# Full-width value products with a block of ones beside V, row sums on the other partition half, and reordered first pairs, in a banded-attention and feed-forward kernel

## The chip, the cores and the metric

One core of one Trainium2 chip. The metric is the time in microseconds (us) of one execution of the whole program, as the device measures it. Where a ratio is given, it is the mean time of one kernel's fast runs over the mean time of the other's in the same rounds on the same chip, with a 95% interval; it is therefore not quite the ratio of the medians that are quoted beside it. Single figures such as "the logarithm took 714 ns" are from one profiled execution of the kernel named.

## The reference, cut to what matters

```python
def _attn_ref(q, k, v, global_idx):        # B=8, H=8, S=576, D=64, 8 global positions
    scores = (1 / np.sqrt(D)) * np.matmul(q, k.transpose(0, 1, 3, 2))
    mask = np.abs(pos[:, None] - pos[None, :]) <= 32           # a band ...
    mask = mask | is_global[:, None] | is_global[None, :]      # ... and global rows, columns
    scores = np.where(mask, scores, -1e9)
    attn = np.exp(scores - np.max(scores, axis=-1, keepdims=True))
    attn = attn / (np.sum(attn, axis=-1, keepdims=True) + 1e-09)
    return np.matmul(attn, v)

def _moe_ref(x, w_in, w_out, s, b):        # 4608 tokens, 512 -> 2048 -> 512
    r = np.maximum(x @ w_in, 0.0)
    g = s * (r * r) + b
    return g @ w_out                       # x is the attention's output, heads side by side
```

## The kernel before

The attention runs over 32 pairs of heads (eight batches, four pairs each). Each pair passes eight steps. In steps 0 to 4 one of five chunks of keys is handled: a score matmul `pss`, an exponential `e` on ScalarE, a masked product `em` on VectorE. In step 6 come the value products `po`. The normalisation of that pair then runs inside the chunks of the *next* pair: a logarithm `ln` of the row sums at step 1, its reciprocal exponential `rep` at step 3, and the product `xt` on VectorE in step 4. Between all this, one "quantum" of feed-forward work per step fills TensorE: 16 quanta `psh` (products with `w_in`, each evicted by a ReLU on ScalarE and squared on VectorE), then 16 quanta `pso` (products with `w_out`), of which every fourth is evicted. From pair 9 on the pairs take turns in this: two that run mostly `psh`, two that run mostly `pso`.

```python
def pv(p, parts=(0, 1)):                       # value products, 28 matmuls, 64 columns wide
    for part in parts:                         # part 0: V, part 1: row sums
        for c in range(NCH):
            for a, n, x in pieces(part * LQ, c):
                for hh in range(2):            # the two heads of the pair
                    nc.tensor.matmul(
                        po[D * hh : D * hh + D, a : a + n],
                        onesb[:] if part else vring[:, p % NV, c, hh],
                        emt[(p, c)][:, hh, x : x + n], ...)

def norm_steps(p):
    def sums():                                # attention of the global rows
        nc.vector.tensor_reduce(out=gs[:, hp], in_=..., axis=AX.X, op=OP.add)
        ...
    def s1():
        nc.scalar.activation(ln[:], po[:, LQ : 2 * LQ], AF.Ln)          # 128 x 640
        later.append(sums)
    def s2():
        nc.scalar.activation(rep[:], ln[:], AF.Exp, scale=-1.0)
        later.append(lambda: nc.vector.tensor_tensor(                   # 128 x 600
            out=view(xt[:, hp, x0:], ...), in0=halves(po[:, 0:LQ]),
            in1=halves(rep[:]), op=OP.mult))
    return [s1, s2]

def run_pair(p, nq, extra):
    for s in range(8) if p > 4 else range(NCH, 8):
        prev, later[:] = list(later), []
        if s < NCH:
            qk(p, s)                           # pss, e; em goes to `later`
            if s in (1, 3):
                step()                         # s1 at step 1, s2 at step 3
        ...
        elif s == 6:
            pv(p)
            pending.extend(norm_steps(p))
        for f in prev:                         # VectorE work of the step before
            f()
        if s == 6 and p + 1 < NSIX:
            put_v(None, p + 1)                 # the global rows of V, by SyncE's DMA queue
        for f in extra.get(s, ()):             # adds and releases: one at step 4, ...
            f()
        Q(nq[s])                               # a quantum of the feed-forward
```

The `po` tile has one buffer: the value products of a pair may not start before the `xt` of the pair ahead has read it.

The softmax here doesn't subtract the row's maximum and nothing guards it: scores larger than these inputs give would overflow.

## Time and profile before

| | before |
|---|---|
| median of 3 runs | 378.12 us (377.26 to 379.49) |
| span of the profiled run | 377.1 us |
| TensorE, VectorE, ScalarE busy | 91%, 63%, 61% |
| a pair in the middle, from its last value product to that of the next pair | 9.02 us, most of them; 9.3 to 9.9 us where `psh` runs |

Two more views are needed later. The first is the page's account of the chain of work that ended last, by engine and by line. It reads backwards from the last instruction, always to what released it: in nearly two thirds of the time the end waited for TensorE.

```profile
PE 63%; ACT 10%; issue 8%; DVE 8%; DMA 5%; POOL 3%; SPq 1%; POOLq 0%; ACTq 0%; DVEq 0%
```

The second is the cost of the two instructions that the change splits, from the page's groups (line, engine, operation, output and inputs, count, total busy us, mean ns, idle time before).

```profile
L539 DVE TENSOR_TENSOR xt<-po,rep 128x600 bf16<-128x600 f32 x32 | 25.0, 782 | 6.1 <-ACT rep L537 5.4
...
L533 ACT ACTIVATE ln<-po 128x640 f32<-128x640 f32 x32 | 22.8, 714 | 1.9 <-PE po L502 1.7
```

### The profile page before, as it was taken

Reading aid. Unit: us, or ns where it says so; the run is one execution under the profiler, and the core shown is the slowest. Engines: PE = TensorE matmul, PEld = TensorE weight load, DVE = VectorE, ACT = ScalarE, POOL = GpSimd, SP = SyncE. Lnnn points to the kernel's source line nnn. Section 1 sums busy time; section 2 is a strip of 40 time slices with the busy share of each in tenths; the row PEclk is TensorE's granted clock in tenths of the full one; section 3 lists DMA queues with packets and bytes.
Section 4 is the critical chain, followed back from the end, with each engine's and each line's share of the span. In section 5 each row is a group of like instructions: output and inputs, shape, how many; then the busy total and the mean of one; then the engine's idle time right before and its main releaser. Section 6 shows DMA issues by size and latency. Waiting matters only on the chain.

```text
span 377.1 us, 7687 instructions
## 1 busy us (share of the span) xinstructions
PE 342.7 (91%) x2707; PEld 183.3 (49%) x2743; DVE 238.5 (63%) x634; ACT 228.8 (61%) x441; POOL 74.9 (20%) x156
## 2 busy tenths in 40 slices
PE   4777697389999999999999999999999999999995
PEld 1344443235545554556765555555556754444442
DVE  3667756357788879866776786667656753432421
ACT  8448767375588458745874687479658841611610
POOL 6664193102213331011202110201020010000000
PEclk9969989889999999999999999999999999999999
DMA  7999489979878866659976998786424002002002
GB/s 133 201 211 217 74 139 212 192 162 180 176 159 190 191 161 117 119 129 209 191 167 146 214 202 136 169 188 124 107 91 71 2 28 86 0 29 85 1 28 83
DMA packets 125831, 50.15 MB, mean 133 GB/s; under 512 B 113512, under 2 KB 118632, under 8 KB 125792
## 3 DMA queue, kind: packets, MB, share of 16 engines
q1 hardware_dynamic: 117040, 37.34, 49.0%
q0 software_dynamic: 8544, 12.03, 16.0%
q8 instruction: 21, 0.34, 0.4%
q10 hardware_dynamic: 208, 0.29, 0.3%
q14 instruction: 18, 0.15, 0.1%
HBM read 42.26 MB, written 9.44 MB: 137 GB/s over the span
## 4 chain that ended last, share of the span: by engine, by line
PE 63%; ACT 10%; issue 8%; DVE 8%; DMA 5%; POOL 3%; SPq 1%; POOLq 0%; ACTq 0%; DVEq 0%
PE pso L588 31%; PE psh L573 21%; PE po L502 6%; PE pss L476 4%; ACT r L580 4%; DMA natv<-in_v_dram 3%; DVE g L583 2%; ACT e L480 2%; ACT rep L537 1%; PE pst L196 1%; DVE em L483 1%; DMA vring<-gvx 1%; DMA wst<-in_moe_w_out_dram 1%; ACT qbd L231 1%; DVE xt L539 1%
## 5 line engine op out<-in xcount | busy, mean ns | idle before, releaser
L573 PE MATMUL psh<-xt,win_t 128*128 128x512 bf16 (+4 forms) x690 | 141.7, 344 | 2.3 <-POOL xt L550 1.0
L588 PE MATMUL pso<-wout_t,g 128*128 128x512 bf16 x559 | 135.7, 379 | 2.0 <-issue 1.6
L580 ACT ACTIVATE r<-psh 128x512 bf16<-128x512 f32 x144 | 89.3, 620 | 64.1 <-PE psh L573 62.6
L480 ACT ACTIVATE e<-pss 128x384 bf16<-128x384 f32 (+1 forms) x160 | 77.0, 488 | 62.6 <-PE pss L476 62.6
L573 PEld LDWEIGHTS <-win_t 128*128 128x128 bf16 x704 | 64.9, 99 | 57.0 <-issue 5.6
L583 DVE TENSOR_TENSOR g<-r 128x512 bf16<-128x512 bf16 x144 | 62.6, 435 | 35.4 <-ACT r L580 33.3
L588 PEld LDWEIGHTS <-g 128*128 128x128 bf16 x576 | 54.8, 98 | 59.5
L483 DVE TENSOR_TENSOR em<-e,mask 128x384 bf16<-128x384 bf16 (+1 forms) x160 | 57.0, 357 | 18.5 <-ACT e L480 17.6
L476 PE MATMUL pss<-qbd,kt 128*128 128x384 bf16 (+1 forms) x160 | 50.7, 321 | 5.7 <-DVE qbd L428 2.4
L602 DVE SCALAR_TENSOR_TENSOR osb<-pso,s_bc,bias_row 128x512 f32<-128x512 f32 x28 | 21.0, 750 | 38.1 <-PE pso L588 38.1
L550 POOL COPY xt<-xg 128x4 bf16 x64 | 14.6, 229 | 115.1 <-DVE xt L539 111.4
L216 POOL CAST vring<-natv 128x640 bf16<-128x640 f32 x24 | 17.7, 739 | 69.8 <-DMA natv<-in_v_dram 21.8
L502 PE MATMUL po<-em,vring 128*64 128x160 bf16 (+3 forms) x448 | 21.9, 229 | 8.0 <-DMA vring<-gvx 6.1
L539 DVE TENSOR_TENSOR xt<-po,rep 128x600 bf16<-128x600 f32 x32 | 25.0, 782 | 6.1 <-ACT rep L537 5.4
L502 PEld LDWEIGHTS <-vring 128*64 128x64 bf16 x448 | 17.0, 113 | 19.8 <-issue 9.1
L476 PEld LDWEIGHTS <-kt 128*128 128x128 bf16 x160 | 15.7, 99 | 20.4 <-DVE qbd L428 5.5
L537 ACT ACTIVATE rep<-ln 128x640 f32<-128x640 f32 x32 | 24.4, 762 | 0.0
L533 ACT ACTIVATE ln<-po 128x640 f32<-128x640 f32 x32 | 22.8, 714 | 1.9 <-PE po L502 1.7
L204 DVE COPY qbd<-pst 64x600 bf16<-64x600 bf16 x48 | 22.3, 465 | 0.3
L502 PE MATMUL po<-em,onesb 128*64 128x160 bf16 (+2 forms) x448 | 19.9, 225 | 0.0
L465 DVE COPY qbd<-pst 64x600 bf16<-64x600 bf16 x8 | 6.2, 774 | 21.1 <-ACT qbd L465 21.1
L182 ACT CAST natbk<-natk 120x640 bf16<-120x640 f32 x24 | 18.2, 760 | 0.0
(99 smaller groups left out, 224.5 us busy)
## 6 DMA issues: line engine op xcount, KB each, us to landing
natv<-in_v_dram SPq DMA_DIRECT2D x55, 150.0 KB
out_dram<-osb SPq DMA_DIRECT2D x28, 256.0 KB
natk<-in_k_dram SPq DMA_DIRECT2D x47, 150.0 KB
natq<-in_q_dram SPq DMA_DIRECT2D x47, 150.0 KB
wst<-in_moe_w_out_dram POOLq DMA_DIRECT2D x8, 512.0 KB, 6.5
win_t<-in_moe_w_in_dram POOLq DMA_DIRECT2D x2, 1024.0 KB
wout_t<-in_moe_w_out_dram POOLq DMA_DIRECT2D x4, 512.0 KB
out_dram<-osbh SPq DMA_DIRECT2D x8, 256.0 KB
```

What stands on the lines that cost most here:

```text
L204: nc.vector.tensor_copy(out=view(qbufs[p % 3][r, hh], [P, NCH], [HB + NG, 2], [1, HB]), in_=view(ps[r], [P, NCH], [HB, 2], [1, HB]),)
L476: nc.tensor.matmul(ps[:], ktile[p][:, P * c : P * c + P], qbufs[p % 3][:, :, LO[c] : HI[c]])
L480: nc.scalar.activation(e[:], ps[:], AF.Exp, scale=SCALE)
L483: later.append(lambda: nc.vector.tensor_mul(em[:], e[:], masks[c]))
L502: nc.tensor.matmul(po[D * hh : D * hh + D, a : a + n], onesb[:] if part else vring[:, p % NV, c, hh], emt[(p, c)][:, hh, x : x + n], start ...
L533: nc.scalar.activation(ln[:], po[:, LQ : 2 * LQ], AF.Ln)
L537: nc.scalar.activation(rep[:], ln[:], AF.Exp, scale=-1.0)
L539: lambda: nc.vector.tensor_tensor(out=view(xt[:, hp, x0:], [KC, NCH], [HB, 2], [1, HB]), in0=halves(po[:, 0:LQ]), in1=halves(rep[:]), op=O ...
L573: nc.tensor.matmul(psh[:, d0 : d0 + n], win_t[:, a, f * P : f * P + P], xt[:, a, x0 : x0 + n], start=(a == 0 and j == 0), stop=(a == 3), s ...
L580: nc.scalar.activation(r[:], psh[:], AF.Relu)
L583: later.append(lambda g=g, r=r: nc.vector.tensor_mul(g[:], r[:], r[:]))
L588: nc.tensor.matmul(pso[:], gl[f][:, u * P : u * P + P], wout_t[:, f], start=(f == 0), stop=(f == 15),)
```

## The change

Its intent: of the 28 half-width matmuls of a pair's value products, half compute only row sums. If each head's stationary operand holds its 64 columns of V *and* 64 columns of ones, 14 full-width matmuls give both, and TensorE need not switch its tiling for them. Head 0 has the ones first, so its values land on partitions 64 to 127 and its row sums on 0 to 63; head 1 the other way round. The heads thus lie swapped by halves, which swapped rows of `w_in` undo. The price: the row sums of a head lie on the other half than its values, and in other columns for the two heads, so the logarithm and `xt` each become two instructions on 64 partitions. So do the small reciprocal and product of the global rows, which VectorE does once for a batch, in the first pair of the next one.

```diff
-    vring = const.tile([P, NV, NCH, 2, D], BF16)
+    vring = const.tile([P, NV, NCH, 2, 2 * D], BF16)
...
-        for part in parts:
+        for hh in parts:
             for c in range(NCH):
-                for a, n, x in pieces(part * LQ, c):
-                    for hh in range(2):
-                        nc.tensor.matmul(
-                            po[D * hh : D * hh + D, a : a + n],
-                            onesb[:] if part else vring[:, p % NV, c, hh], ...
+                for a, n, x in pieces(hh * LQ, c):
+                    nc.tensor.matmul(
+                        po[:, a : a + n], vring[:, p % NV, c, hh], emt[(p, c)][:, hh, x : x + n], ...
...
+        own = [slice(D, P), slice(0, D)]
         def s1():
-            nc.scalar.activation(ln[:], po[:, LQ : 2 * LQ], AF.Ln)
+            for hh in range(2):
+                nc.scalar.activation(
+                    ln[own[hh]], po[own[1 - hh], LQ * hh : LQ * hh + LQ], AF.Ln
+                )
...
+            def scaled():
+                for hh in range(2):
+                    nc.vector.tensor_tensor(
+                        out=view(xt[own[hh], hp, x0:], ...),
+                        in0=halves(po[own[hh], LQ * hh : LQ * hh + LQ]),
+                        in1=halves(rep[own[hh]]), op=OP.mult,
+                    )
```

The rest, in short: `w_in` is loaded in four pieces with its halves swapped; the start is reordered (q is rounded before buffers are cleared, the band is built by GpSimd, the global rows are evicted by ScalarE); in pairs 5 to 7 the global V rows are put in place by VectorE instead of by a transfer; and three feed-forward quanta move from the tail into batch 1:

```diff
             if s == 6 and p + 1 < NSIX:
-                put_v(None, p + 1)
+                put_v(V, p + 1)
...
-            nq = [0, 1, 1, 1, 0, 1, 1, 1] if hp else [0, 0, 0, 0, 0, 0, 1, 2]
+            nq = [0, 1, 1, 1, 0, 1, 1, 2] if hp else [0, 0, 0, 0, 0, 0, 1, 2]
```

More of the change, by code (lines that the diff above doesn't have):

```diff
@@ L215, in cast_v @@
     def cast_v(eng, p):
-        eng(out=vring[:, p % NV], in_=natv[:, p % NV])
+        eng(
+            out=view(vring[:, p % NV, 0, 0, D:], [4 * D, NCH], [1, 2 * D]),
+            in_=natv[:, p % NV].rearrange("p c h d -> p c (h d)"),
+        )
     nc.scalar.add_instruction(
@@ L231, in clear @@
         nc.scalar.copy(out=ap, in_=view(zero[0 : ap.shape[0]], [0, n]))
-    for t in qbufs[:2]:
-        clear(t[0:D, 1], LQ)
-        clear(t[D:P, 0], LQ)
-    clear(natv[0:NG].rearrange("p n c h d -> p (n c h d)"), NV * NCH * 2 * D)
-    clear(qbufs[2][0:D, 1], LQ)
-    clear(qbufs[2][D:P, 0], LQ)
+    nc.vector.memset(qbufs[0][0:D, 1], 0.0)
+    nc.vector.memset(qbufs[0][D:P, 0], 0.0)
+    nc.scalar.copy(out=six["q"][:NP6, 0].rearrange("p h j d -> p (h j d)"), in_=six0["q"])
     for t in "kq":
@@ L246 @@
     nc.vector.memset(half[D:P], float(S))
-    onesb = const.tile([P, D], BF16)
-    nc.vector.memset(onesb[:], 1.0)
     load_v(nc.sync, 0)
@@ L272 @@
     )
+    nc.vector.tensor_copy(
+        out=six["k"][:NP6, 0].rearrange("p h j d -> p (h j d)"), in_=six0["k"]
+    )
+    for t in qbufs[1:]:
+        nc.vector.memset(t[0:D, 1], 0.0)
+        nc.vector.memset(t[D:P, 0], 0.0)
     grow = [const.tile([P, 1], mybir.dt.uint32, name=f"grow{i}", tag=f"grow{i}") for i in range(4)]
@@ L283 @@
     rows_of(0)
-    nc.vector.tensor_copy(
-        out=six["k"][:NP6, 0].rearrange("p h j d -> p (h j d)"), in_=six0["k"]
-    )
-    nc.scalar.copy(out=six["q"][:NP6, 0].rearrange("p h j d -> p (h j d)"), in_=six0["q"])
     gfs = {}
@@ L326 @@
         nc.gpsimd.memset(t[0:NG, WIN : WIN + P], 1.0)
+    nc.gpsimd.memset(kidx[0:NG], 100000.0)
+    nc.gpsimd.memset(iot[:, GAP : GAP + NG], 100000.0)
+    band = const.tile([P, WM], FP32)
+    nc.gpsimd.tensor_tensor(out=band[:], in0=iot[:], in1=iot[:], op=OP.mult)
+    nc.gpsimd.tensor_scalar(
+        out=band[:], in0=band[:], scalar1=(float(WIN) + 0.5) ** 2, scalar2=None, op0=OP.is_le
+    )
     gather(0, "kqv")
@@ L343 @@
     for j in range(2):
-        nc.gpsimd.dma_start(
-            out=win_t[:, :, 1024 * j : 1024 * j + 1024],
-            in_=w_in2[:, :, 1024 * j : 1024 * j + 1024],
-        )
+        for hh in range(2):
+            f = slice(1024 * j, 1024 * j + 1024)
+            r, o = slice(D * hh, D * hh + D), slice(D - D * hh, P - D * hh)
+            nc.gpsimd.dma_start(out=win_t[o, :, f], in_=w_in2[r, :, f])
         if j == 0:
@@ L387, in evac @@
             def evac():
-                nc.vector.tensor_copy(out=gkt[bb][:], in_=ps[:, 0])
+                eng = nc.vector.tensor_copy if bb else nc.scalar.copy
+                eng(out=gkt[bb][:], in_=ps[:, 0])
                 for hh in range(2):
                     r = slice(D * hh, D * hh + D)
-                    nc.vector.tensor_copy(out=gqd[bb % 2][r, hh], in_=ps[r, 1])
+                    eng(out=gqd[bb % 2][r, hh], in_=ps[r, 1])
             later.append(evac)
@@ L404, in move @@
             later.append(
-                lambda: nc.vector.tensor_copy(
+                lambda: nc.scalar.copy(
                     out=gvx[bb][:, 512 * i : 512 * i + 512],
@@ L417, in put_v @@
         (eng or nc.sync.dma_start)(
-            out=vring[0:NG, p % NV].rearrange("g c h d -> g c (h d)"),
+            out=view(vring[0:NG, p % NV, 0, 0, D:], [4 * D, NCH], [1, 2 * D]),
             in_=view(g, [0, NCH], [1, 2 * D]),
@@ L496, in pv @@
         po, started = otile[p]
-        for part in parts:
+        for hh in parts:
             for c in range(NCH):
-                for a, n, x in pieces(part * LQ, c):
-                    for hh in range(2):
-                        key = (a // 512, hh)
-                        nc.tensor.matmul(
-                            po[D * hh : D * hh + D, a : a + n],
-                            onesb[:] if part else vring[:, p % NV, c, hh],
-                            emt[(p, c)][:, hh, x : x + n],
-                            start=key not in started, stop=(part == 1 or c == NCH - 1),
-                            skip_group_check=True,
-                        )
-                        started.add(key)
+                for a, n, x in pieces(hh * LQ, c):
+                    key = a // 512
+                    nc.tensor.matmul(
+                        po[:, a : a + n], vring[:, p % NV, c, hh], emt[(p, c)][:, hh, x : x + n],
+                        start=key not in started, stop=(hh == 1 or c == NCH - 1),
+                        skip_group_check=True,
+                    )
+                    started.add(key)
     def norm_steps(p):
@@ L528, in sums @@
                 xgs[bi] = xg
-                nc.vector.reciprocal(out=rec[:], in_=gs[:, :, 1])
-                nc.vector.tensor_tensor(out=xg[:], in0=gs[:, :, 0], in1=rec[:], op=OP.mult)
+                for hh in range(2):
+                    nc.vector.reciprocal(out=rec[own[hh]], in_=gs[own[1 - hh], :, hh])
+                for hh in range(2):
+                    nc.vector.tensor_tensor(
+                        out=xg[own[hh]], in0=gs[own[hh], :, hh], in1=rec[own[hh]], op=OP.mult
+                    )
         def s1():
-            nc.scalar.activation(ln[:], po[:, LQ : 2 * LQ], AF.Ln)
+            for hh in range(2):
+                nc.scalar.activation(
+                    ln[own[hh]], po[own[1 - hh], LQ * hh : LQ * hh + LQ], AF.Ln
+                )
             later.append(sums)
@@ L537, in s2 @@
             nc.scalar.activation(rep[:], ln[:], AF.Exp, scale=-1.0)
-            later.append(
-                lambda: nc.vector.tensor_tensor(
-                    out=view(xt[:, hp, x0:], [KC, NCH], [HB, 2], [1, HB]),
-                    in0=halves(po[:, 0:LQ]), in1=halves(rep[:]), op=OP.mult,
-                )
-            )
+            def scaled():
+                for hh in range(2):
+                    nc.vector.tensor_tensor(
+                        out=view(xt[own[hh], hp, x0:], [KC, NCH], [HB, 2], [1, HB]),
+                        in0=halves(po[own[hh], LQ * hh : LQ * hh + LQ]),
+                        in1=halves(rep[own[hh]]), op=OP.mult,
+                    )
+            later.append(scaled)
         return [s1, s2]
@@ L745 @@
     warm(4)
-    nc.vector.memset(kidx[0:NG], 100000.0)
-    nc.vector.memset(iot[:, GAP : GAP + NG], 100000.0)
-    band = const.tile([P, WM], FP32)
-    nc.vector.tensor_scalar(
-        out=band[:], in0=iot[:], scalar1=-float(WIN) - 0.5, scalar2=None, op0=OP.is_ge
-    )
-    nc.vector.scalar_tensor_tensor(
-        out=band[:], in0=iot[:], scalar=float(WIN) + 0.5, in1=band[:],
-        op0=OP.is_le, op1=OP.mult,
-    )
-    flush()
+    clear(natv[0:NG].rearrange("p n c h d -> p (n c h d)"), NV * NCH * 2 * D)
     cast_v(A, 0)
+    nc.vector.memset(view(vring[:, 0, 0, 0], [4 * D, NV * NCH], [3 * D, 2], [1, D]), 1.0)
     vkey = const.tile([P, NCH], FP32)
@@ L775 @@
     nc.vector.tensor_tensor(out=notg[:], in0=vkey[:], in1=isg[:], op=OP.is_gt)
+    flush()
     build_masks((0, 1))
```

## The prediction

> **What bounds the kernel now.** I read the window table first, cut at the stages that the code has: start-up, first pairs, the four pairs of batch 1, the long middle, the last pairs, the feed-forward tail. Columns are window, length, busy us of the five engines (PEld apart), clock, DMA share, GB/s.
>
> ```profile
> 0.00:24.50 24.50, 14.38 (x130) 6.77 (x134) 14.67 (x57) 14.28 (x20) 15.63 (x33) 0.92 1.03 177
> 24.50:45.60 21.10, 16.10 (x237) 9.46 (x235) 14.49 (x42) 16.78 (x34) 6.43 (x9) 0.93 0.95 168
> 45.60:94.00 48.40, 36.95 (x298) 18.99 (x302) 28.52 (x79) 28.43 (x55) 17.75 (x32) 0.89 0.98 172
> 94.00:233.10 139.10, 136.52 (x1111) 76.36 (x1124) 107.53 (x278) 98.62 (x199) 26.68 (x55) 1.00 0.81 168
> 233.10:305.40 72.30, 71.43 (x613) 40.85 (x619) 49.09 (x134) 50.12 (x101) 6.81 (x21) 1.00 0.47 102
> 305.40:377.10 71.70, 67.34 (x331) 30.91 (x336) 24.18 (x49) 20.55 (x34) 1.62 (x8) 0.99 0.12 45
> ```
>
> From 94 us on, TensorE is busy 98% of the time; before that about three quarters. So removing matmul work should count late, removing waits early. But the busy share hides what the value products cost, so I went to the timeline of TensorE around one of them, then to the same place in a pair where ScalarE evicts all eight quanta:
>
> ```profile
> 167.56 1.03 PE L588 MATMUL pso<-wout_t,g 128*128 128x512 bf16 x4
> 168.52 0.61 PE L502 MATMUL po<-em,vring 128*64 128x160 bf16 x14
> 168.96 0.59 PE L502 MATMUL po<-em,onesb 128*64 128x160 bf16 x14
> 169.71 0.38 PE L588 MATMUL pso<-wout_t,g 128*128 128x512 bf16 x1 [0.16 <-issue]
> ```
> ```profile
> 112.98 0.28 PE L502 MATMUL po<-em,vring 128*64 128x32 bf16 x4 [0.42 <-DVE em L483]
> 113.06 0.61 PE L502 MATMUL po<-em,onesb 128*64 128x160 bf16 x14
> ```
>
> Here 28 half-width matmuls run from 168.52 to about 169.38: the two halves are already concurrent, because one after the other they would need twice that. Four 512-column matmuls step by 0.215 us, so the first value product could start at 168.42 and the next quantum at 169.38; they start at 168.52 and 169.71. The bubbles are about 0.10 and 0.33 us, 0.42 us a pair. In the second fence TensorE had to wait for the last masked chunk `em`: there VectorE, not TensorE, paces the pair. ScalarE and VectorE of such a pair:
>
> ```profile
> 218.93 0.51 ACT L480 ACTIVATE e<-pss 128x384 bf16<-128x384 f32 x1
> 219.30 0.73 ACT L533 ACTIVATE ln<-po 128x640 f32<-128x640 f32 x1
> 219.88 0.64 ACT L580 ACTIVATE r<-psh 128x512 bf16<-128x512 f32 x1
> ...
> 221.60 0.80 ACT L537 ACTIVATE rep<-ln 128x640 f32<-128x640 f32 x1
> ```
> ```profile
> 222.43 0.78 DVE L539 TENSOR_TENSOR xt<-po,rep 128x600 bf16<-128x600 f32 x1 [0.26 <-ACT rep L537]
> 223.13 0.41 DVE L583 TENSOR_TENSOR g<-r 128x512 bf16<-128x512 bf16 x1
> 223.46 0.69 DVE L834 TENSOR_TENSOR osbh<-osbh,bias_row 128x512 f32<-128x512 f32 x1
> 224.06 0.32 DVE L483 TENSOR_TENSOR em<-e,mask 128x320 bf16<-128x320 bf16 x1
> ```
>
> ScalarE has no gap here: each starts before the one ahead of it has ended. The chain is logarithm, reciprocal exponential `rep`, product `xt`, bias add, last `em`, value product. The start-to-start cost of the logarithm is 0.58 us, of `xt` 0.70 us. Last, the waits show one early stall:
>
> ```profile
> 67.21 0.45 PE L441 MATMUL pst<-ident,sixk 96*64 96x96 bf16 x12
> 68.23 0.45 PE L441 MATMUL pst<-ident,sixq 96*64 96x96 bf16 x12 [0.57 <-ACT e L480]
> 73.99 1.01 PE L502 MATMUL po<-em,vring 128*64 128x160 bf16 x14 [5.31 <-DMA vring<-gvx]
> 74.79 1.01 PE L502 MATMUL po<-em,onesb 128*64 128x160 bf16 x14
> 76.13 0.63 PE L573 MATMUL psh<-xt,win_t 128*128 128x512 bf16 x1 [0.33 <-issue]
> ```
>
> TensorE is ready at 68.7 us and waits until 74.0 for the few global V rows, whose tiny transfer stands in SyncE's queue behind the loads of later pairs. Afterwards it runs at the low clock: the 14 matmuls take 1.01 instead of 0.61 us, a 512-column one 0.63 instead of 0.38.
>
> **What the Trainium skill says.** TensorEngine Tiling (Array Packing), section Key Properties: changing the tiling mode drains TensorE; the trace agrees, 0.42 us of bubbles a pair where a 128*64 group stands between 128*128 ones. ScalarE: Activation LUTs, section What ACT_TABLE_LOAD costs: time follows elements per lane, 186 ns + 0.833 N, with about 93 ns overlap; 719 ns for N = 640 agrees with the logarithm's mean of 714 ns in the groups, and the 64-row clearing of the same length took 722 ns. So half the partitions cost as much as all. VectorE: DVE Perf Modes, section Two Vector instructions with no wait between them: an instruction whose start quadrant differs from the last one's is held until the earlier ones finish; the trace agrees, the two 64-row copies to `qbd` in a pair step by their full 0.47 us while 128-row operations overlap by 0.08.
>
> **The change, part by part.**
>
> *Value products.* Per pair 28 half-width matmuls and 28 loads become 14 and 14 at full width. The columns that stream are the same: 2 x (160 + 3 x 192 + 160) = 1792, 0.75 us at the 0.215 us per 512 of the trace. The gain is thus not half of the 41.8 us that the two groups show (21.9 + 19.9) but the two switches: about -0.42 us a pair where TensorE sets the pace. With 23 pairs from 94 us on, at most -10 us.
>
> *Normalisation.* Row sums lie on the other 64 rows, so each logarithm and each `xt` is two half-row instructions. ScalarE: +1 logarithm per pair, +0.62 us (0.714 - 0.093). VectorE: +1 `xt`, +0.78 and the lost overlap 0.08, +0.87 us. Two more reciprocals and products per batch, +0.54 us per four pairs.
>
> Pairs that evict `psh` throughout (two of four in a tile of 32 quanta): both additions lie in the dense chain: +0.62 + 0.87 = +1.49, less 0.42, about +1.1 us. Pairs that run `pso`: ScalarE has room; the value product waits for the last `em`, which today has 0 to 0.42 us of slack while wsum or bias additions run: +0.87 + 0.10 - slack gives a wait of 0.55 to 0.97 against 0.42 saved: +0.1 to +0.5. The last eight pairs have no such additions and about 1 us of slack in the `pso` pairs: -0.4 each. Moving three quanta aligns the `psh` phase to whole pairs, so the first of the two starts without backlog: I count it at half. Middle, pairs 8 to 23: 4 x (1.1 + 0.5) + 8 x 0.3 = +8.8; last eight: 4 x -0.4 + 2 x 0.9 = about 0. I take +7, since some backlog drains under `pso` quanta.
>
> *Global rows for pairs 5 to 7 by VectorE* instead of a transfer (0.46 us, as the one such copy takes): removes the 5.3 us wait, and about 2 us of slow clock after it: -7.3. Three pairs in this stage pay the extra logarithm and `xt`: +3.3. Sum -4.
>
> *Quanta.* Three more are done in batch 1, where TensorE is idle a quarter of the time. The tail runs quanta of four 512-column matmuls at 0.86 us: -2.6.
>
> *Start-up.* Before, ScalarE clears 64-row buffers and the natural V rows for 7 us before it rounds q; q now goes first, band goes to GpSimd (-0.8 on VectorE), V's global rows are evicted by ScalarE (-1.3). Against it: the VectorE clears of 0.33 us each, and one memset of ones over 2560 bf16 columns, which at the 0.83 ns per element of the existing memsets is 2.2 us ahead of the masks. Net about -2. Each of the four first pairs is bound by ScalarE's and VectorE's chain and pays about +0.9, less 0.4 for the two bubble pairs: +2.
>
> *w_in rows and GpSimd.* Four loads instead of two, 0.85 us more issue each; first used at 47 us, so hidden.
>
> Sum: +7 - 4 - 2.6 - 2 + 2 = +0.4, so 378.5. These terms are large and of both signs; I lean by 1.5 us to the faster side, since the early gains are waits that disappear for certain. Predicted: 377 us.
>
> **Rivals.** (a) TensorE stays the bound and everything else hides: 23 pairs x -0.42, plus -4, -2.6: about 361. For it: 98% busy, ScalarE 71% and VectorE 77% busy between 94 and 233 us. Against: averages; the dense stretch and the 0.42 us wait on `em` show no room in half of the pairs. (b) The chain takes all of it: nothing drains, both `psh` pairs pay 1.1 and the `pso` pairs 0.5: middle +13, total about 385. For it: with one bias add of 0.69 us, `psh` pairs last 9.3 to 9.6 us against 9.02 elsewhere, so the chain is elastic to additions. (c) The early wait moves: without its own transfer, the pair's next limit is the transposed keys of pair 8 on the same queue. The DMA engines are full there (share 1.2 from 58 to 74 us), so -4 could shrink to 0: about 381.
>
> **Range and chances.** (a) in part against (b) in part gives 367 to 387. Faster than 370.6 needs most pairs to hide the extra instructions: 0.23. Slower than 385.7 needs (b) or (c) whole: 0.17. Within 2%: 0.60.
>
> **What would show it.** The bubbles around the value products should vanish: the last product to the next quantum about 0.07 us instead of 0.39. The logarithm should appear 64 times at about 0.71 us, `xt` 64 times at about 0.78. Pairs with `psh` should grow to about 10 us with TensorE waiting for `em`; late `pso` pairs should fall to about 8.6. The wait at 68 us should be gone. If half-row instructions cost less than full ones, or if `em` stays early, I am wrong towards (a); if a transfer wait reappears before 90 us, towards (c).

## The result, and the profile after

The changed kernel takes 414.05 us (median of 4 runs, 412.24 to 416.37) against 378.81 us for the kernel before in the same rounds; the ratio is 1.0935 [1.0858, 1.1013]: slower, far outside the range of the prediction.

The windows of the changed kernel, cut at the same points of the program (the first value product of pairs 0, 4, 8, 23 and 31). As in the prediction's first fence the columns are window, length, busy us (and count) of TensorE, its weight loads (PEld), VectorE, ScalarE and GpSimd, clock, DMA share, GB/s:

```profile
0.00:22.50 22.50, 16.20 (x131) 6.98 (x132) 15.92 (x54) 11.70 (x19) 14.61 (x34) 1.00 0.96 169
22.50:49.10 26.60, 15.34 (x178) 8.90 (x176) 18.33 (x47) 19.87 (x37) 9.78 (x13) 0.98 0.90 153
49.10:97.10 48.00, 39.38 (x259) 19.82 (x260) 31.33 (x86) 31.74 (x59) 17.21 (x31) 0.94 0.96 174
97.10:259.40 162.30, 138.84 (x914) 76.74 (x915) 120.85 (x301) 111.64 (x214) 29.44 (x57) 1.00 0.67 144
259.40:341.60 82.20, 73.11 (x507) 41.38 (x508) 55.79 (x146) 56.09 (x108) 7.04 (x21) 1.00 0.39 90
341.60:411.30 69.70, 65.02 (x310) 29.72 (x309) 25.41 (x52) 21.24 (x35) 1.61 (x8) 0.99 0.12 46
```

In the middle, which is now 162 instead of 139 us long, TensorE is busy 86% of the time (138.84 of 162.30) where it was 98%. Note that neither ScalarE (69%) nor VectorE (74%) is anywhere near full. No engine is the bound; a chain across engines is. The page says so as well:

```profile
PE 33%; DVE 19%; ACT 17%; issue 16%; DMA 7%; POOL 4%; SPq 1%; POOLq 1%; DVEq 0%; ACTq 0%
```

The starts of the last value product of pairs 0, 4, 8, 24 and 31 in the two traces cut the span into stages (us):

| stage | before | after | difference |
|---|---|---|---|
| start to pair 0 | 27.41 | 24.83 | -2.6 |
| pairs 1 to 4 | 18.97 | 25.62 | +6.7 |
| pairs 5 to 8 | 48.44 | 48.42 | 0.0 |
| pairs 9 to 24 | 148.37 | 172.42 | +24.1 |
| pairs 25 to 31 | 63.06 | 71.65 | +8.6 |
| tail | 70.82 | 68.31 | -2.5 |
| span | 377.07 | 411.25 | +34.2 |

So most of the loss is in pairs 9 to 31, 1.42 us each (32.6 / 23). Pairs 1 to 4 add 6.7, start and tail give 5.1 back, and pairs 5 to 8, where the early wait went, come out even. The groups name the two instructions that were split:

```profile
L557 DVE TENSOR_TENSOR xt<-po,rep 64x600 bf16<-64x600 f32 x64 | 49.9, 780 | 7.4 <-ACT rep L553 6.7
...
L547 ACT ACTIVATE ln<-po 64x640 f32<-64x640 f32 x64 | 44.7, 698 | 4.1 <-PE po L511 3.0
```

Twice as many, and each half costs what the whole did: 780 ns against 782, 698 against 714. Now the same place in a `psh` pair as in the prediction, first ScalarE, then VectorE:

```profile
113.61 0.51 ACT L490 ACTIVATE e<-pss 128x384 bf16<-128x384 f32 x1
114.14 1.41 ACT L547 ACTIVATE ln<-po 64x640 f32<-64x640 f32 x2
115.57 0.60 ACT L600 ACTIVATE r<-psh 128x512 bf16<-128x512 f32 x1
...
117.28 0.76 ACT L553 ACTIVATE rep<-ln 128x640 f32<-128x640 f32 x1
```
```profile
118.08 1.57 DVE L557 TENSOR_TENSOR xt<-po,rep 64x600 bf16<-64x600 f32 x2 [0.26 <-ACT rep L553]
119.58 0.41 DVE L603 TENSOR_TENSOR g<-r 128x512 bf16<-128x512 bf16 x1
119.91 0.68 DVE L835 TENSOR_TENSOR wsum<-wsum,wst 128x512 f32<-128x512 f32 x1
120.51 0.31 DVE L493 TENSOR_TENSOR em<-e,mask 128x320 bf16<-128x320 bf16 x1
```

From the start of the logarithm to that of the next instruction it is now 1.43 us (115.57 - 114.14); it was 0.58. From the start of `xt` to the next, 1.50 us (119.58 - 118.08); it was 0.70. What follows on TensorE:

```profile
119.80 0.48 PE L511 MATMUL po<-em,vring 128*128 128x160 bf16 x5 [0.89 <-DVE xt L557]
120.87 0.65 PE L511 MATMUL po<-em,vring 128*128 128x32 bf16 x9 [0.60 <-DVE em L493]
121.36 0.38 PE L593 MATMUL psh<-xt,win_t 128*128 128x512 bf16 x1
```

TensorE first waits 0.89 us until `xt` has let go of the single `po` buffer, does five products, and waits another 0.60 us for the last `em`. Both waits stand in the list of waits of the whole run (engine and what it waited for, total us, times, longest); ahead of them the ones of before, and in both lists other waits stand between those shown:

```profile
DVE gs L520 <- ACT ln L533: 5.0, 21, 0.4
...
PE pss L476 <- ACT e L480: 2.3, 5, 0.5
...
PE po L502 <- DVE em L483: 1.2, 4, 0.4
```
```profile
DVE gs L529 <- ACT ln L547: 29.2, 31, 1.1
...
PE po L511 <- DVE xt L557: 19.2, 28, 1.5
...
PE po L511 <- DVE em L493: 14.3, 21, 1.0
...
PE pss L486 <- ACT e L490: 10.3, 17, 1.4
```

The largest of those shown, the reduction `gs` on VectorE waiting for the logarithms, grew from 5.0 to 29.2 us. It is the first suspect only to the eye: whether it stands on the chain or beside it is one of the questions below.

### The profile page after: what moved, and what is told of

Its sections match the earlier page's. It is cut to its first block, busy times and chain, and to the rows that moved or that the text cites. A ratio compares the mean times of both kernels' runs of the same rounds, so it can differ in the third digit from the quotient of the medians.

```text
span 411.2 us, 6906 instructions
## 1 busy us (share of the span) xinstructions
PE 347.9 (85%) x2295; PEld 183.5 (45%) x2295; DVE 267.6 (65%) x682; ACT 252.3 (61%) x472; POOL 79.7 (19%) x162
## 4 chain that ended last, share of the span: by engine, by line
PE 33%; DVE 19%; ACT 17%; issue 16%; DMA 7%; POOL 4%; SPq 1%; POOLq 1%; DVEq 0%; ACTq 0%
PE pso L608 16%; PE psh L593 12%; DVE xt L557 7%; ACT e L490 5%; ACT ln L547 4%; ACT r L600 3%; PE po L511 3%; ACT rep L553 3%; DMA natv<-in_v_dram 2%; DVE em L493 2%; DVE g L603 2%; DMA natq<-in_q_dram 2%; DVE osb L622 2%; PE pss L486 1%; DVE osbh L846 1%
## 5 line engine op out<-in xcount | busy, mean ns | idle before, releaser
L593 PE MATMUL psh<-xt,win_t 128*128 128x512 bf16 (+2 forms) x704 | 141.9, 343 | 2.3 <-ACT r L600 1.8
L608 PE MATMUL pso<-wout_t,g 128*128 128x512 bf16 x576 | 138.6, 379 | 0.0
L490 ACT ACTIVATE e<-pss 128x384 bf16<-128x384 f32 (+1 forms) x160 | 73.7, 474 | 65.4 <-PE pss L486 64.7
L511 PE MATMUL po<-em,vring 128*128 128x160 bf16 (+3 forms) x448 | 37.1, 221 | 34.8 <-DVE xt L557 19.2
L557 DVE TENSOR_TENSOR xt<-po,rep 64x600 bf16<-64x600 f32 x64 | 49.9, 780 | 7.4 <-ACT rep L553 6.7
L511 PEld LDWEIGHTS <-vring 128*128 128x128 bf16 x448 | 29.4, 98 | 49.3 <-issue 42.8
L547 ACT ACTIVATE ln<-po 64x640 f32<-64x640 f32 x64 | 44.7, 698 | 4.1 <-PE po L511 3.0
L529 DVE TENSOR_REDUCE gs<-po 128x16 f32<-128x80 f32 x32 | 7.7, 241 | 29.2 <-ACT ln L547 29.2
L206 DVE COPY qbd<-pst 64x600 bf16<-64x600 bf16 x48 | 22.3, 464 | 0.3
L717 PE MATMUL psw<-dummy 128*128 128x512 bf16 x37 | 16.6, 512 | 1.3 <-DVE dummy L233 1.3
```

What stands on the lines that cost most here:

```text
L490: nc.scalar.activation(e[:], ps[:], AF.Exp, scale=SCALE)
L511: nc.tensor.matmul(po[:, a : a + n], vring[:, p % NV, c, hh], emt[(p, c)][:, hh, x : x + n], start=key not in started, stop=(hh == 1 or c ...
L547: nc.scalar.activation(ln[own[hh]], po[own[1 - hh], LQ * hh : LQ * hh + LQ], AF.Ln)
L557: nc.vector.tensor_tensor(out=view(xt[own[hh], hp, x0:], [KC, NCH], [HB, 2], [1, HB]), in0=halves(po[own[hh], LQ * hh : LQ * hh + LQ]), in ...
L593: nc.tensor.matmul(psh[:, d0 : d0 + n], win_t[:, a, f * P : f * P + P], xt[:, a, x0 : x0 + n], start=(a == 0 and j == 0), stop=(a == 3), s ...
L608: nc.tensor.matmul(pso[:], gl[f][:, u * P : u * P + P], wout_t[:, f], start=(f == 0), stop=(f == 15),)
```

## The experiments

Three theories. **A**: the split of the logarithm and of `xt` into halves makes the whole loss, because they stand on the chain from one value product to the next. **B**: the full-width products themselves, with their stationary operands of 128 columns or their layout, cost the time. **C**: the reordering (start, global rows by VectorE, moved quanta) costs it. Within A the mechanism is open too: is it the added busy time of ScalarE and VectorE, the place of the added work, or the wait of the reduction?

### The two halves of the change

`e1_values_only` is the kernel before with only the value products, ones, half-row normalisation and `w_in` changed. `e2_early_only` is the complement: the reordered start, VectorE's global rows and the moved quanta, with the old value products.

> The kernel before with only the full-width value products, V beside ones, the half-row normalisation and the w_in swap; start-up order, the transfer of the global rows and the quanta stay as before. Theory A (the two half-row logarithms and the two half-row products lengthen the chain of every pair): the loss of 35 us stays whole and the early savings are missing, so 412 to 420 us, pairs 8 to 31 at about 10.6 us each. Rival B (the reordered start, the moved quanta and the global rows on VectorE lose the time): 370 to 385 us.

> The kernel before with everything of the change but the value products and their normalisation: reordered start, band on GpSimd, global rows of pairs 5 to 7 by VectorE, three quanta earlier. Theory A: faster than before, 368 to 374 us (the 5.3 us wait and the slow clock after it go, the start gains about 2 us, the tail 2.6). Rival B: slower than before, 385 us or more.

Both correct. `e1_values_only` took 420.37 us, ratio 1.11 [1.1042, 1.1157]; `e2_early_only` 371.49 us, ratio 0.9779 [0.9719, 0.9839] (378.96 for the kernel before in those rounds). (The first lies just above the 412 to 420 us expected.) So +41.4 and -7.5 us, together +33.9, which is the change's +35.2 within the spread. C falls: the reordering is a gain, hidden under the loss of the other half.

### The split alone, and everything but the split

`e4_halves_old` takes the kernel before, with its old value products and layout, and merely issues each logarithm and each `xt` as two instructions of 64 partitions, which compute the same:

```diff
-            nc.scalar.activation(ln[:], po[:, LQ : 2 * LQ], AF.Ln)
+            for r in (slice(D, P), slice(0, D)):
+                nc.scalar.activation(ln[r], po[r, LQ : 2 * LQ], AF.Ln)
...
+                for r in (slice(D, P), slice(0, D)):
+                    nc.vector.tensor_tensor(
+                        out=view(xt[r, hp, x0:], ...), in0=halves(po[r, 0:LQ]), in1=halves(rep[r]), ...
```

`e3_one_norm` is the reverse: the changed kernel, with one 128-row pass and one 128-row `xt` in place of the halves. Its numbers are wrong (the row sums of the wrong head meet the values). The pass is an identity function instead of a logarithm, since values, not row sums, stand in half of its rows, and these can be negative. It takes as long as the logarithm did (711 ns against 714 in the groups of the two runs).

```diff
-            for hh in range(2):
-                nc.scalar.activation(
-                    ln[own[hh]], po[own[1 - hh], LQ * hh : LQ * hh + LQ], AF.Ln
-                )
+            nc.scalar.activation(ln[:], po[:, LQ : 2 * LQ], AF.Identity)
...
-                for hh in range(2):
-                    nc.vector.tensor_tensor(out=view(xt[own[hh], ...]), ...)
+                nc.vector.tensor_tensor(out=view(xt[:, hp, x0:], ...), in0=halves(po[:, 0:LQ]), ...)
```

> The kernel before, right numbers, half-width value products as they were, but logarithm and product each split into two 64-row instructions. Theory A: this alone makes nearly all of the loss, and the bubbles stay: 405 to 420 us. Rival C: 380 to 390 us.

> The changed kernel with the full-width value products kept, but one 128-row pass of ScalarE in place of the two half-row logarithms and one 128-row product in place of two: the numbers come out wrong on purpose (the pass is an identity, since it would take the logarithm of negative values). Theory A: the loss goes and the saved bubbles show, 358 to 370 us, TensorE-bound pairs at 8.5 to 8.7 us. Rival C (the full-width products themselves, or the doubled V tile, are what is slow): above 395 us.

`e4_halves_old`: correct, 414.51 us, ratio 1.0933 [1.0872, 1.0995]. The split alone, with no other part of the change, costs 35.6 us, as much as the whole change loses. That the two agree so closely is partly chance: the change also has the early gains (-7.5 us), and full width with its layout adds some 6 us to the split (420.37 against 414.51; more below). `e3_one_norm`: 369.35 us, ratio 0.9732 [0.9675, 0.979]; without the split the change would be a gain. B falls, and A holds in both directions.

`e3_one_norm` also prices the prize. Its pairs that TensorE paces last 8.76 us against 9.02 before, so full width is worth 0.26 us in such a pair (`e2_early_only`, which has everything of the change but full width and the split, has 9.02 there too); over the whole kernel it ended only 2.1 us ahead of `e2_early_only` (369.35 against 371.49), and the intervals of those two ratios overlap.

### Which of the two

`e5_ln_halves` splits only the logarithm, `e6_xt_halves` only `xt`, each in the kernel before.

> The kernel before with the logarithm alone split into two 64-row instructions, the product left whole. The split costs ScalarE 1.43 us where the whole one took 0.58 from start to start. Theory A (in-order chains): this delays each later exponential, reciprocal and the reduction on VectorE, so +15 to +22 us: 393 to 401. If only the busy time counted (rival D: ScalarE has a third of its time free), +0 to +5 us.

> The kernel before with the product xt alone split into two 64-row instructions, the logarithm left whole. Theory A: +0.8 us on VectorE in front of the last masked chunk in every pair, less the slack that some pairs have: +10 to +18 us, 389 to 397. Rival D: +0 to +5 us. The two splits together made +36 us; if they add up, the two runs share that.

Both correct. The logarithm: 391.74 us, ratio 1.0328 [1.0302, 1.0353], +12.7 us over 379.06. `xt`: 394.44 us, ratio 1.0418 [1.0377, 1.0459], +15.4 us. Together 28.1, against 35.6 us with both. (For the logarithm +15 to +22 us was expected; it fell short.) The traces say where the sum fails, from the lengths of single pairs. In pair 10, with eight ReLUs, the logarithm's split adds 0.81 us, that of `xt` 0.79 and both 1.60: they add up. In pair 12, which runs `pso`, the three are 0.30, 0.51 and 1.21. That fits a slack in the `pso` pairs that either one alone partly uses up.

### Busy time, or its place on the chain

`e8_off_chain` adds to the kernel before the same two instructions in each pair from 4 on, but off the chain: at step 6, behind the value products, from a constant into scratch that nobody reads.

```diff
+    def off_chain():
+        z = view(zero[D:P], [0, NCH], [0, 2], [0, HB])
+        nc.scalar.activation(spare_a[D:P], view(zero[D:P], [0, LQ]), AF.Identity)
+        nc.vector.tensor_tensor(out=halves(spare_v[D:P]), in0=z, in1=z, op=OP.mult)
...
+        at(6, off_chain)
```

> The kernel before plus, in each of the 28 pairs from pair 4, one extra 64-row pass on ScalarE and one extra 64x600 product on VectorE into scratch, issued behind the value products, where ScalarE idles 1.3 us: the same extra instructions in kind and length as the split makes, off the chain. Theory A: +0 to +8 us. Rival D' (the engines' total work is what counts): near the +36 us of the split, scaled to 28 pairs, over 400 us.

Correct, 379.05 us, ratio 0.9994 [0.9964, 1.0025]: nothing. That the work was done, the groups of this run show; it is 42.5 us of busy time:

```profile
L843 DVE TENSOR_TENSOR spare_v<-zero 64x600 bf16<-64x600 f32 x28 | 22.0, 784 | 0.9
...
L842 ACT ACTIVATE spare_a<-zero 64x640 f32<-64x640 f32 x28 | 20.5, 732 | 0.7
```

Nearly the same busy time (46.8 us over all 32 pairs in `e4_halves_old`) costs 35.6 us in one place, 29.6 of them in pairs 9 to 31, and nothing in another. A caution that the run carries itself: the extra instructions read a constant and not `po`, so they differ from the halves in what they depend on as well as in place. That is what "off the chain" means, but it is why the next experiment was needed, which moves the real ones.

`f1_moved` is the changed kernel with the real halves moved from pair 4 on: both logarithms right behind the value products at step 6, where ScalarE waits anyway; `rep` at step 0; the halves of `xt` in two steps, with other work between.

```diff
             if s < NCH:
                 qk(p, s)
-                if s in (1, 3):
+                if s == 0:
                     step()
...
                 pv(p)
-                pending.extend(norm_steps(p))
+                s1, s2 = norm_steps(p)
+                s1()
+                pending.append(s2)
```

> The changed kernel with the same instructions, but from pair 4 on the two logarithms are issued directly behind the pair's value products (where ScalarE idles about 2 us), the reciprocal at step 0 of the next pair instead of 3, and the two products xt at steps 1 and 2 instead of both in front of the last masked chunk. Right numbers. Theory A: most of the loss goes, 366 to 380 us, TensorE-bound pairs at 8.76 us as in the run with one normalisation. If the instructions' number and not their place is what costs: above 400 us.

Correct, 374.82 us, ratio 0.9899 [0.9836, 0.9961]. It has all 64 logarithms and all 64 `xt` and still takes 39 us less than the change (374.82 against 414.05). ScalarE in one of its pairs:

```profile
213.65 0.60 ACT L603 ACTIVATE r<-psh 128x512 bf16<-128x512 f32 x1
214.47 1.41 ACT L547 ACTIVATE ln<-po 64x640 f32<-64x640 f32 x2 [0.22 <-PE po L511]
215.90 0.60 ACT L603 ACTIVATE r<-psh 128x512 bf16<-128x512 f32 x1
```

The two logarithms still take 1.41 us and still do not overlap; they now fall where what stands behind them holds TensorE up far less (pairs 9 to 24 take 9.29 us each, where the change takes 10.78). So it was the place, not the amount. The move shifts logarithms, `rep` and `xt` at once; which of the three mattered most is not separated.

### The largest wait

`e9_sums_first` puts the reduction `gs` ahead of the logarithms, so that VectorE's 29.2 us of waiting for them go away.

> The changed kernel with the reduction of the global columns on VectorE issued before the logarithms instead of behind them. In the trace of the changed kernel VectorE idles 29.2 us in 31 waits of that reduction for the second logarithm. If these waits are on the chain: up to 25 us less, 388 to 400. If they only stand beside ScalarE's own delay of the exponentials: 408 to 415 us.

Correct, 411.62 us, ratio 1.0869 [1.0823, 1.0915], beside the change's 1.0935 with an interval that overlaps: 2.4 us of 35 by the medians. The traces show where it acts. Pairs 12, 16, 20, 24 and 28, in which the batch's reciprocals and products follow the reduction, are 0.48 us shorter each (in pair 12 10.65 to 10.17), which is about what pairs 9 to 31 gain in all (244.07 to 241.72); the others keep their lengths (11.21 in pair 10). So for the most part this wait stood beside the chain, and on it only once in four pairs.

### What the other parts do, and a better kernel

`e7_early_no_shift` is `e2_early_only` without the three moved quanta.

> The early parts alone as run before (371.5 us), but without the three quanta moved to batch 1. In that run the tail was 2.4 us shorter and pairs 8 to 24 took 9.48 us each against 9.27 before. If the move is what lengthens those pairs, they return to 9.27 and the tail grows by 2.4: 369.5 to 372.5 us in all, a wash. If they stay at 9.48, about 374.

Correct, 368.87 us, ratio 0.9741 [0.9707, 0.9775], against 0.9779 [0.9719, 0.9839] with them. Moving the quanta gains nothing: the traces show the tail 2.6 us shorter (68.43 against 71.01), but pairs 9 to 24 longer, 9.48 against 9.35 us each, and pairs 5 to 8 too (42.72 against 39.30). What was saved later was paid earlier.

The chains above suggested one more change. The adds of `wsum` and the releases of `osbh` are issued at step 4, so on VectorE they stand between `xt` and the last `em`, on the chain. `g1_adds_later` is `e7_early_no_shift` with those moved by one step:

```diff
-            for s in (4, 7):
+            for s in (5, 7):
                 if adds:
                     at(s, adds.pop(0))
...
-            at(4, release)
+            at(5, release)
```

`b1_early_adds` has this and, besides, VectorE in place of the transfer for the global V rows of the first pairs; `f2_early_moved` is that with the early logarithm of `f1_moved`; `g2_moved_adds_later` is `f1_moved` with the adds moved (it keeps the moved quanta, since without them, as its expectation says, this order deadlocks).

> The best run so far (the kernel before with the early parts, no quanta moved, 368.9 us) plus the global rows of pairs 1 to 4 by VectorE too, and the bias and w_out-sum additions issued one step later, behind the last masked chunk instead of in front of it. Theory A: the eight psh pairs of 8 to 24 that take 9.3 to 9.9 us fall towards 9.02: 4 to 5 us less, and the start perhaps 1: 362 to 366 us. If those additions are not on the chain: 367 to 370 us.

> The run before this one plus the logarithm issued directly behind the value products and the reciprocal at step 0, with the whole 128-row instructions of the kernel before. If the chain still binds the psh pairs after the additions moved: 1 to 3 us less than that run; if TensorE sets the pace by then (9.02 us a pair): the same within 1 us.

> The early parts alone without moved quanta (368.9 us), plus only the bias and w_out-sum additions one step later; the global rows of pairs 1 to 4 stay a transfer. In the run that did both, pairs 8 to 24 fell from 9.35 to 9.12 us each but value product 8 came 6 us later. If the copies on VectorE in the first pairs made that delay: 363 to 366 us. If the later additions made it: 368 to 371 us.

> The changed kernel with its normalisation moved off the chain (374.8 us), plus the additions one step later; quanta moved as in the change, since without that move this order deadlocks. If the additions still bound its psh pairs: pairs 8 to 24 fall from 9.29 towards 8.8 us each, 366 to 370 us, which would make the full-width products worth about 0.26 us a pair against the half-width ones. If not: 373 to 376 us.

All correct:

| run | median us | ratio | pairs 9 to 24, us each | start to pair 8, us |
|---|---|---|---|---|
| `e7_early_no_shift` | 368.87 | 0.9741 [0.9707, 0.9775] | 9.35 | 82.40 |
| `b1_early_adds` | 369.90 | 0.9779 [0.9739, 0.9819] | 9.12 | 88.58 |
| `f2_early_moved` | 370.26 | 0.9783 [0.9749, 0.9818] | 9.12 | 90.98 |
| `g1_adds_later` | 366.32 | 0.9689 [0.9663, 0.9715] | 9.12 | 84.09 |
| `g2_moved_adds_later` | 371.13 | 0.9803 [0.9763, 0.9842] | 9.07 | 90.69 |

The kernel before has 9.27 us and 94.82 us in the last two columns. `g1_adds_later` beats both kernels by a clear margin, 3.1% faster than before. Over `e7_early_no_shift`, from which it differs by the adds alone, it gains 2.5 us by the medians; the two intervals just overlap, but its trace puts 3.8 us in pairs 9 to 24 (145.86 against 149.62), the stage that the move touches. The early logarithm of `f2_early_moved` earned nothing there (9.12 with and without it). In the trace of `g1_adds_later` the last `em` follows `xt` at once, and the add comes behind it:

```profile
219.05 0.78 DVE L549 TENSOR_TENSOR xt<-po,rep 128x600 bf16<-128x600 f32 x1 [0.26 <-ACT rep L547]
219.75 0.32 DVE L493 TENSOR_TENSOR em<-e,mask 128x320 bf16<-128x320 bf16 x1
219.98 0.69 DVE L835 TENSOR_TENSOR osbh<-osbh,bias_row 128x512 f32<-128x512 f32 x1
```

With full width on top (`g2_moved_adds_later`) the middle is as good or a little better, and its pairs that TensorE paces last 8.76 us, but it reaches pair 8 some 6.6 us later, and it missed the 366 to 370 us expected for it. Its pairs 0 to 3 still have the split in the old place.

`b1_early_adds` was a miss: moving the first pairs' V rows to VectorE as well made the way to pair 8 longer, not shorter. The trace of `b1_early_adds` shows VectorE's copies waiting 4.3 us there for ScalarE's rounding of V, but why it costs this much was not settled. The start is also the stage where single profiles scatter most: `e2_early_only`, `e7_early_no_shift` and `g1_adds_later` have the same code up to pair 0 and reach its last value product at 24.18, 22.17 and 20.98 us. So differences of 3 us in the last column say little; that of the medians, 3.6 us between `b1_early_adds` and `g1_adds_later`, is larger than their spread.

## Why the prediction was wrong, point by point

By its own terms, with the stages of the table above:

| term of the sum | forecast | measured |
|---|---|---|
| start | -2 | -2.6 |
| first pairs | +2 | +6.7 |
| batch 1 (wait removed, three pairs split) | -4 | 0.0 |
| middle, pairs 9 to 24 | +7 | +24.1 |
| last pairs | about 0 | +8.6 |
| moved quanta, tail | -2.6 | -2.5 |

The start is a hit partly by luck: single profiles of the same start lie up to 3 us apart (above).

**What was right.** That columns stream the same and little but the switches is saved (size below); that a half costs what a whole does; that both additions lie on the chain in `psh` pairs; that the early wait goes. The changed kernel around 75 us, where TensorE had waited 5.31 us:

```profile
74.46 0.45 PE L451 MATMUL pst<-ident,sixq 96*64 96x96 bf16 x12 [0.91 <-ACT e L490]
75.25 1.22 PE L511 MATMUL po<-em,vring 128*128 128x160 bf16 x14 [0.35 <-DVE xt L557]
76.31 1.89 PE L593 MATMUL psh<-xt,win_t 128*128 128x512 bf16 x8
```

Pairs 5 to 8 without the split took 39.30 us (`e7_early_no_shift`) against 48.44 before; with the split, the full width and the quanta the gain was gone again. Rival (c), that a transfer wait would take the place of this one, is not what happened; rival (b), the chain, is what happened, at nearly twice the size that it was given in the middle (+13 forecast, +24.1 measured), and with +8.6 us in the last pairs besides.

**Step 1 that failed: "+0.62 us (0.714 - 0.093)".** This took the overlap of 93 ns from the Trainium skill's page ScalarE: Activation LUTs (section What ACT_TABLE_LOAD costs), which the prediction cites, and let it hold for halves. It does not: two logarithms take 1.41 us and the next instruction starts 0.02 us after their end, so the step is 1.43 us, and the addition +0.85. The trace of before had shown it, in the clearing of buffers by alternating 64-row halves on ScalarE:

```profile
2.62 2.93 ACT L231 CAST qbd<-zero 64x640 bf16<-64x640 f32 x4
```

Four take 2.93 us, 0.73 each, with no overlap. The prediction read the duration of one from this line (722 ns) and not the distance from one to the next. The rule that it cites for VectorE (VectorE: DVE Perf Modes, section Two Vector instructions with no wait between them), that a change of the start quadrant holds the next instruction, would describe ScalarE here as well. In `e4_halves_old` the second half starts at partition 0 like the instruction after it, and here the overlap is back at that end:

```profile
284.75 1.41 ACT L534 ACTIVATE ln<-po 64x640 f32<-64x640 f32 x2
286.06 0.58 ACT L584 ACTIVATE r<-psh 128x512 bf16<-128x512 f32 x1
```

The step is 1.31 us, where the change, whose second logarithm reads partitions 64 to 127 and writes 0 to 63, has 1.43. This fits; no run tested the rule by itself. `xt` was sized well: +0.87 forecast, +0.80 measured (1.50 - 0.70).

**Step 2 that failed: "less 0.42, about +1.1 us" in `psh` pairs.** In a pair of eight ReLUs, the way from the logarithm's start to the end of `rep` went from 3.10 to 3.90 us, and from there to the end of the last `em` from 1.98 to 2.78: +1.60 together, and the pair from 9.61 to 11.21. Nothing was to be deducted, since TensorE waits for that `em` in any case. And the credit was too large. Of the 0.42 us, 0.33 were a gap between the last row-sum product and the next quantum, which is mostly a record that the trace lacks. At another such place of the kernel before, the weight loads and the matmuls:

```profile
160.46 1.41 PEld L588 LDWEIGHTS <-g 128*128 128x128 bf16 x8
```
```profile
160.69 1.67 PE L588 MATMUL pso<-wout_t,g 128*128 128x512 bf16 x7 [0.16 <-issue]
```

Eight loads, but seven matmuls: the first one's record is missing, and the "gap" is where it ran. (Over the run there are 576 loads of this line and 559 matmuls.) In `e2_early_only`, with the same half-width products and no record missing, the last row-sum product is followed by the next quantum after 0.17 us in every pair from 8 on, and not 0.39; with full width after 0.07. In the pairs that TensorE paces, `e3_one_norm` saves against it 0.09 us on the way in, 0.10 on the way out and 0.05 within the group (0.80 to 0.75 from its first product to its last). So the two switches were worth about 0.19 us, and full width as a whole the 0.26 by which the pair got shorter, 9.02 to 8.76.

**Step 3 that failed, the largest: "Pairs that run `pso`: ScalarE has room", +0.1 to +0.5, and "the last eight pairs ... about 1 us of slack".** ScalarE did have room: in `pso` pairs `rep` ends 2.93 us after the logarithm's start, where it was 2.78. It is VectorE's *order* that had none. In the `pso` pair at 178 us of the changed kernel, VectorE idles 1.08 us until the logarithms end; what it used to do in that time then stands before or behind `xt`:

```profile
179.80 0.24 DVE L529 TENSOR_REDUCE gs<-po 128x16 f32<-128x80 f32 x1 [1.08 <-ACT ln L547]
180.08 0.72 DVE L539 RECIPROCAL rec<-gs 64x32 f32<-64x32 f32 x2
180.83 0.41 DVE L541 TENSOR_TENSOR xg<-gs,rec 64x32 bf16<-64x32 f32 x2
...
181.81 1.58 DVE L557 TENSOR_TENSOR xt<-po,rep 64x600 bf16<-64x600 f32 x2
183.31 0.73 DVE L622 SCALAR_TENSOR_TENSOR osb<-pso,s_bc,bias_row 128x512 f32<-128x512 f32 x1
183.97 0.67 DVE L846 TENSOR_TENSOR osbh<-osbh,bias_row 128x512 f32<-128x512 f32 x1
184.57 0.31 DVE L493 TENSOR_TENSOR em<-e,mask 128x320 bf16<-128x320 bf16 x1
```

`rep` had ended at 181.29 (180.55 and 0.74 us long). `xt` starts 0.52 us later instead of 0.03, its step is 0.80 longer, and the eviction `osb`, which ran ahead of `xt` in the like pair of before, now lies behind it with 0.66. That makes 1.95, and the last `em` ends 3.59 us after `rep` where it ended 1.65 after it. (In `e4_halves_old`, with its quanta not moved, the same pairs have 3.15: `xt` 0.71 later and 0.80 longer.) Up to pair 23 a `pso` pair of the change lasts 10.15 to 10.66 us; it was to be 9.1 to 9.5. From pair 24 on it lasts 9.56 to 10.05; it was to be 8.6. `e9_sums_first` says what the wait of 1.08 us itself is worth: with the reduction ahead, `xt` starts 0.03 us after `rep` again and this pair is 0.49 us shorter. So that part of the 1.95 came from the late reduction and the small instructions behind it, and the rest did not. The prediction had worked out two more reciprocals and products a batch ("+0.54 us per four pairs") and then left them out of its sum. Two chains meet in a `pso` pair, the exponentials held up behind two logarithms and `xt` held up on VectorE; their shares are known only for the split in the kernel before (0.30, 0.51 and both 1.21 in pair 12, above).

**Step 4 that failed: "less 0.4" and "+2" for the first pairs.** Pairs 1 to 4 lost 6.7 us, not 2. `e4_halves_old` loses 5.8 in them (24.72 against 18.97), so here too it is the split. In the change the wait of TensorE for an exponential that stands behind the logarithms went from 0.51 to 1.36 us (at 33.8 us in either trace), by the same 0.85 as the logarithm's step.

`e1_values_only` is some 6 us slower than `e4_halves_old` (420.37 against 414.51). Its traces put 2.5 of them in pairs 9 to 31, and there 0.42 or 0.43 each in pairs 12, 16, 20, 24 and 28: behind the reduction stand two reciprocals and two products (0.73 and 0.40 us) where `e4_halves_old` has one of each (0.35 and 0.19), and `xt` starts 1.17 us after `rep` instead of 0.74. This is a price of the layout that the split of logarithm and `xt` does not contain. Another 1.7 us lie in the start, where VectorE writes the columns of ones for 2.19 us; no run tested that alone.

What stays open: the rest of that difference; why VectorE's V rows in the first pairs cost time; and whether full width could win if pairs 0 to 3 were reordered as well.

## What to carry to other kernels

Ask of an added instruction not how busy its engine is, but what stands behind it in that engine's order: 42.5 us of additional ScalarE and VectorE work cost nothing behind the value products, and 36 us between an exponential and the product that TensorE waited for. Before a layout is taken that makes one full-height instruction into two of half height, price it as two whole ones, and weigh that against what is really saved (here 0.26 us a pair against 1.4). And when part of a change is bad, look what the rest is worth by itself: the reordered first pairs, with the additions one step later, gave 3.1%.

## What the Trainium skill lacked or had wrong

- ScalarE: Activation LUTs, section What ACT_TABLE_LOAD costs, has back-to-back instructions overlap by about 93 ns. Here two 64-row logarithms on different partition halves take 1.41 us at a mean of 698 ns, and four clearings of alternate halves 2.93 us at 722 ns each: no overlap, where a whole logarithm overlapped the next instruction by 0.15 us (0.73 long, 0.58 from start to start). The holding rule for a changed start quadrant stands only on VectorE: DVE Perf Modes (Two Vector instructions with no wait between them); these numbers would fit it on ScalarE too.
- Perfetto Trace Analysis, section Optimizing Scalar/DVE Operations, says that where Scalar and Vector are not saturated but cause bubbles elsewhere, breaking up instructions may let work be completed sooner. It does not say along which axis. Breaking them up by partitions did the opposite at 61% and 63% busy: each half took as long as the whole, +35.6 us (`e4_halves_old`).
- TensorEngine Tiling (Array Packing), section Key Properties, says that a change of the tiling mode drains TensorE, without a size. Here the two changes around a group of 28 matmuls were worth about 0.19 us a pair (0.09 and 0.10), and full width as a whole 0.26 (9.02 to 8.76).
- Perfetto Trace Analysis does not say that a gap ahead of a matmul can be a matmul whose record is missing; comparing the loads and matmuls of a line shows it (576 against 559 here).
